# Pair 8's scores ahead of block 1's first tiles, and two pairs in a load

## The chip, the cores and the metric

The kernel runs on one core of a Trainium2 chip. The metric is the device time of one execution in microseconds. Before the change it was 324.54 us, the median of three runs (321.65, 324.54 and 325.66).

The core has five engines with an instruction queue each: TensorE (PE; its weight loads are shown apart, as PEld), VectorE (DVE), ScalarE (ACT), GpSimd (POOL) and SyncE (SP). Each runs its own instructions in order and waits on semaphores for the others. Loads from memory are issued from POOL's queue, because they turn float32 into bfloat16 on the way; stores and DMA transposes are issued from SP's.

## The reference

```python
# q, k, v: (8 batches, 8 heads, 576 positions, 64)
scores = (q @ k^T) / 8, kept where 0 <= query - key < 64, else -1e9
attn = softmax(scores)                      # rows; exp, sum, divide
x = (attn @ v) as (4608 tokens, 512)        # heads side by side
h = x @ w_in                                # w_in: 512 x 2048
g = h * clip(h + 3, 0, 6) / 6
out = g @ w_out                             # w_out: 2048 x 512; float32
```

It is a causal attention with a sliding window of 64, and behind it a two-layer network with a hard-swish between the layers.

## The kernel before, in words

**Pairs.** The attention works on pairs of heads: pair t is heads 2g and 2g+1 of batch b, with t = 4b + g, so there are 32. For a pair, `turn(t)` transposes its queries and keys on PE (36 small transposes, L276) into two PSUM banks, the "hosts"; `turned(t, 0)` copies the keys to KT on DVE and `turned(t, 1)` the queries to QT on ACT (both L283). `s_first` (L296) and `s_rest` (L310) multiply keys by queries, `s_first` into the unused end of the hosts of the next pair and `s_rest` into two banks of `ps_t`. `weights` takes the exponentials on ACT (L319, L323) and multiplies them by 0/1 masks of the window: one product into P (L328) and two into Pz (L331). From pair 8 on these products run on POOL; on pairs 4 to 7 on DVE. `pv(t)` (L404) multiplies the weights by V, with a column of ones for the sums; `pv_out(t)` divides (L413 to L428, DVE). Then `x_(t)` brings the result to xT by DMA transposes on SP (L442), or, up to pair 7, `x_turned(t)` by transposes on PE (L457, L459) and a copy on ACT (L463).

**Blocks.** The network works on blocks of 512 tokens. A block has 16 first units, each of four matmuls (L487, one for each group of 128 inputs, g = 0 to 3), a ReLU on ACT (L499) and a product on DVE (L500) that ends in gT; and 16 second units of four matmuls each (L523), every fourth with a copy on ACT (L529) and a store from SP (L531). Input group g of a block comes from the pairs with that g, so the first three matmuls of block 1's units need only pairs 4 to 6, and the fourth needs pair 7.

**PSUM banks.** `ps_t` has three banks, `ps_h` two, `ps_acc` one, and `ps_o` one tile of two banks, which `pair_bank()` also hands out. The hosts stand in `ps_h`. A new tile in a pool waits until the last reader of the tile that held its bank is done.

**The order around the change.** The order is written out by hand. Pairs 4 to 7 (batch 1) are scored and finished in two loops; pair 8's transposes follow (`turn_two(8)`), then what is left of block 0. Then comes the stretch that is changed. In the kernel before it reads: three matmuls each of block 1's units 0, 1 and 2; `x_turned(7)`; three of unit 3; the fourth matmul of all four, with their ReLU and product; then `pads(3)` (small memsets on POOL) and `group(7, 4)`. As pair 7 is finished already, `group(7, 4)` transposes pair 9, scores pair 8 and weaves in four entries of the queue `moe`: units 4, 5 and 6 and one second unit.

From pair 8 on, the loop runs `group(t, n)`: outputs of pair t, transposes of pair t + 2, scores of pair t + 1 with their exponentials and masks, and n entries of `moe`.

**Loads.** `load_qk(b, n, first)` issues a load of k and one of q for n pairs of batch b, from pair `first` on (L119, each on POOL's queue); `load_v` loads V in three parts (L138), and `shift` makes a shifted copy of V with two DMAs on SP (L158, L159). Pairs 8, 9 and 10 are loaded one by one while batch 1 is finished. Pair 11's load stands behind `group(7, 4)`, and so on POOL behind pair 8's masks; the first two parts of batch 3's V follow it. Batch 3's pairs 12 to 15 are loaded one by one behind `group(8)` to `group(11)`, that is, on POOL behind the masks of pairs 9 to 12. From batch 4 on, all four pairs come in one load. A POOL instruction that stands behind a DMA issue waits until the issue is made.

Of the kernel before, what the change touches and what calls it, by code (L numbers as in the profile page):

```python
# [36 lines left out]
def kernel(  # L37
# [10 lines left out]
    B, H, S, _ = q.shape  # L48
    DM, FF = moe_w_in.shape
    NT = B * S  # L50
    NG = H // 2
# [3 lines left out]
    NFC = FF // P  # L55
# [14 lines left out]
    ps_t = ctx.enter_context(tc.tile_pool(name="ps_t", bufs=3, space=PSUM))  # L70
    ps_h = ctx.enter_context(tc.tile_pool(name="ps_h", bufs=2, space=PSUM))
    ps_acc = ctx.enter_context(tc.tile_pool(name="ps_acc", bufs=1, space=PSUM))
# [26 lines left out]
    def load_early_qk(pairs, first=0):  # L99
        if first:  # L100
            tiles = staged[0]
        else:
            both = stage.tile([SP, 2, H, R * D], BF16, name="qk6", tag="qk")
            tiles = [both[:, 0], both[:, 1]]
        h = 2 * first
        for n in pairs:
            for t, src in zip(tiles, (q, k)):
                nc.gpsimd.dma_start(  # L108
                    out=t[:, h : h + 2 * n, :],
                    in_=src[0, h : h + 2 * n].rearrange("h (p r) d -> p h (r d)", r=R),  # L110
                )
            h += 2 * n
        return tiles

    def load_qk(b, n=NG, first=0):
        t = staged[b] if first else stage.tile([P, H, RL * D], BF16, name="qk9", tag="qk")
        hs = slice(2 * first, 2 * (first + n))
        for z, src in enumerate((k, q)):
            nc.gpsimd.dma_start(  # L119
                out=t[halves[z], hs], in_=src[b, hs].rearrange("h (p r) d -> p h (r d)", r=RL)  # L120
            )
        return t
# [8 lines left out]
    def load_v(b, whole=False, part=slice(None)):  # L131
        loads = (
            (0, Un[b % 2][:, 0], 2 * P), (2 * P, Un[b % 2][:, 1], 2 * P),
            *(((W, Us[b % 2][:, 0], 2 * P), (W + 2 * P, Us[b % 2][:, 1], 2 * P)) if whole
              else ((4 * P, Us[b % 2][3 * P // 4 : P, 1], W),)),
        )
        for m, to, n in loads[part]:
            nc.gpsimd.dma_start(  # L138
                out=to[:, :, VO : VO + P],
                in_=v[b, :, m : m + n, :].rearrange("h (p r) d -> p h (r d)", r=2),  # L140
            )
# [127 lines left out]
    def turn(t):  # L269

        b, g = divmod(t, NG)
        hosts[t] = [ps_h.tile([P, 8 * P], BF16, name=name, tag="bk") for name in ("tk", "tq")]
        for r in range(RL):
            for h in range(2):
                for z in range(2):
                    nc.tensor.transpose(  # L276
                        out=hosts[t][z][halves[h], r * W : (r + 1) * W],
                        in_=staged[b][halves[z], 2 * g + h, r * D : (r + 1) * D],
                        identity=ident[halves[z], halves[z]],
                    )  # L280

    def turned(t, z):
        (nc.scalar.copy if z else nc.vector.tensor_copy)(  # L283
            out=(QT[t % 4][:] if z else KT[t % 4][:, W:]).rearrange("q (p r) -> q p r", r=RL),
            in_=hosts[t][z][:, 0:S].rearrange("q (r p) -> q p r", p=W),
        )
# [4 lines left out]
    def s_first(t, host):  # L291

        s = [x[0:D, 6 * P : 8 * P].bitcast(F32).rearrange("p (r w) -> p r w", w=W) for x in hosts[host]]
        for r in range(2):
            for h in range(2):
                nc.tensor.matmul(  # L296
                    s[h][:, r], lhsT=keys(t, h, 0, r), rhs=QT[t % 4][halves[h], 0:W], start=True, stop=True,
                )
        return s

    def s_rest(t):

        ss = [ps_t.tile([P, 2, 2, 2, W], F32, name="s", tag="bk") for _ in range(2)]
        for c in range(2):
            for m in range(2):
                for r in range(2):
                    for h in range(2):
                        for i in range(2):
                            w = 4 * m + 2 * i + 1 + c
                            nc.tensor.matmul(  # L310
                                ss[h][halves[i], c, m, r], lhsT=keys(t, h, W * (w - 1), r),
                                rhs=QT[t % 4][halves[h], w * W : (w + 1) * W], start=True, stop=True,
                            )
        return ss
# [68 lines left out]
    def pv(t, apart=False):  # L383
        b, g = divmod(t, NG)
        if apart:
            o = [ps_h.tile([P, 512], F32, name="ot", tag="bk") for _ in range(2)]
            os_[t] = [x[:].unsqueeze(1) for x in o]
        else:
            both = ps_o.tile([P, 2, 512], F32, name="o", tag="o")
            o = [both[:, i] for i in range(2)]  # L390
            os_[t] = [both[:]]
        un, us, pw = Un[b % 2], Us[b % 2], Pw[t % 4]
        for slot in range(5):
            m, h = divmod(slot, 2)
            for r in range(2):
                c0, v0 = slot * OC + r, VO - 1 + r * (D + 1)
                for c in range(2):
                    for i in range(2):
                        if slot < 4:
                            p, vt, hh = pw[halves[i], h, c, m, r], (us if c else un)[halves[i], m], 2 * g + h  # L400
                        else:
                            p = pw[halves[i], c, 0, 0, r] if i else P0[t % 4][:, c, r]
                            vt, hh = un[halves[i], 0], 2 * g + c
                        nc.tensor.matmul(  # L404
                            o[i][halves[c], c0 : c0 + D + 1], lhsT=p, rhs=vt[:, hh, v0 : v0 + D + 1],
                            start=(r == 0), stop=(r == 1), skip_group_check=True,
                        )
# [128 lines left out]
    moe = deque()  # L536
# [22 lines left out]
    def pair_bank():  # L559
        both = ps_o.tile([P, 2, 512], F32, name="hTo", tag="o")  # L560
        return [both[:, i] for i in range(2)]

    def complete(kb, fcs, pair=()):
        unit, hidden = units[kb]
        for fc in fcs:
            unit(fc, (NG - 1,), act=fc not in pair)
            if fc in pair[1:]:
                for x in pair:
                    hidden(x)
        for _ in fcs:  # L570
            moe.popleft()
# [98 lines left out]
    staged = {0: load_early_qk((1,))}  # L670
# [64 lines left out]
    u = units[0][0]  # L735
# [16 lines left out]
    def group(t, n):  # L752

        if t >= 2 * NG:
            pv(t)
        if t + 2 < T:
            turn(t + 2)
        if t + 1 < T:
            host = t + 2
            if host >= T:  # L760
                hosts[host] = [ps_h.tile([P, 8 * P], BF16, name=name, tag="bk") for name in ("tk", "tq")]
            s = s_first(t + 1, host)
            weights(t + 1, s, s_rest(t + 1))
        if t >= 2 * NG:
            pv_out(t)
        if t + 2 < T:
            turned(t + 2, 0)
        if t >= 2 * NG:
            x_(t)
        weave(2)  # L770
        if t + 2 < T:
            turned(t + 2, 1)
        weave(n - 2)
# [6 lines left out]
    def front(t, host, muls=(nc.gpsimd,) * 3):  # L780
        s = s_first(t, host)
        weights(t, s, s_rest(t), muls)
# [54 lines left out]
    late[0] = 1  # L837
    queue_block(1)
    u, some = units[1][0], range(NG - 1)
    u(0, some, ps_t)  # L840
    u(1, some, ps_t)
    u(2, some, ps_acc)
    x_turned(n + 3)
    u(3, some, to=pair_bank()[0])
    complete(1, range(4))
    f, z = [moe.popleft() for _ in range(NFC - 4)], list(moe)
    moe.clear()
    moe.extend(f[0:3] + z[0:1] + f[3:6] + z[1:2] + f[6:] + [z[2], z[4], z[3]] + z[5:])
    pads(3, nc.gpsimd.memset)
    group(2 * NG - 1, 4)  # L850
    load_qk(2, 1, 3)
    load_v(3, part=slice(0, 2))
    for t in range(2 * NG, T):
        b, g = divmod(t, NG)
        if g == 0 and b > 2:
            queue_block(b - 1, lead=4 if b == 3 else 2)
        group(t, -(-len(moe) // (NG - g)))
        if b + 1 < B:
            if g == 0:
                staged[b + 1] = load_qk(b + 1, NG if b > 2 else 1)  # L860
            elif b == 2:
                load_qk(b + 1, 1, g)
            if b == 2 and g == 0:
                load_v(b + 1, part=slice(2, 3))
            if b > 2 and g == 1:
                load_v(b + 1)
            if g == 1 + (b > 2):
                shift(b + 1)
# [38 lines left out]
```

## Time and profile before

| | |
|---|---|
| median of three runs | 324.54 us |
| the profiled execution | 320.98 us |
| its span, first to last instruction | 319.3 us |
| mean granted clock of TensorE | 0.997 |
| two-pair loads, k and q (batch 1) | 17.5 and 18.6 us from issue to landing, among the weights' loads |
| V, 256 KB | 5.5 us, median |
| xT by DMA transpose | 2.9 and 2.4 us, median |

The KB of a load are those that it writes, in bfloat16. A row of a timeline gives the start, the time from the start to the end of the group, the engine, the line, the operation with its output and inputs, the number of instructions, and in brackets the idle time ahead of it with what ended it. Matmuls are pipelined, so rows overlap a little; the chain of waits counts each stretch of time once.

### The profile page before, as it was taken

To read this page: it belongs to the slowest core of one execution; us is meant where nothing else is said; L and a number is where in the kernel's file an instruction comes from. 1 tells how busy PE (TensorE), PEld (TensorE's weight loads), DVE (VectorE), ACT (ScalarE), POOL (GpSimd) and SP (SyncE) were. 2 spreads that over 40 slices of the span, in tenths; PEclk is the share of its full clock that TensorE was granted. 3 is DMA by queue.
4 is the path that set the end of the run, shared out by engine and by line. 5 is a ranking of instruction groups with operands and counts; after the bars stand their busy time and mean duration, and the time that the engine had idled before them with its cause. 6 is when DMAs were issued, how large, how long until landed. Compare 5 with 4: busy or idle time off the path is not lost.

```text
span 319.3 us, 10688 instructions
## 1 busy us (share of the span) xinstructions
PE 302.0 (95%) x4566; PEld 151.8 (48%) x4608; DVE 181.3 (57%) x415; ACT 184.3 (58%) x345; POOL 124.3 (39%) x168
## 2 busy tenths in 40 slices
PE   7889998998999999999999999999999999999992
PEld 3454454544555455555555555555544444444440
DVE  5766657587737754775377537762776156334200
ACT  2738575586757754776477647764773266454410
POOL 8981206289876335543445345633330000000000
PEclk9999999999999999999999999999999999999998
DMA  6999999939999943994299339934021200100021
GB/s 89 161 210 206 207 192 158 201 51 142 168 140 192 98 118 88 166 130 116 88 158 139 107 100 160 138 105 100 4 69 38 84 33 0 69 33 34 36 75 65
DMA packets 57592, 35.67 MB, mean 112 GB/s; under 512 B 39872, under 2 KB 51648, under 8 KB 57536
## 3 DMA queue, kind: packets, MB, share of 16 engines
q0 software_dynamic: 35904, 18.81, 46.0%
q1 hardware_dynamic: 21632, 16.08, 20.4%
q8 instruction: 38, 0.62, 0.8%
q14 instruction: 18, 0.15, 0.1%
HBM read 37.62 MB, written 9.44 MB: 147 GB/s over the span
## 4 chain that ended last, share of the span: by engine, by line
PE 84%; POOL 5%; DMA 3%; ACT 2%; DVE 2%; issue 2%; POOLq 0%; ACTq 0%; DVEq 0%
PE acc L523 36%; PE hT L487 35%; PE o L404 3%; PE s L310 2%; PE acco L523 2%; PE tk L276 2%; DMA V<-in_v_dram 2%; DMA qk<-in_q_dram 2%; POOL qk L108 2%; POOL Pz L331 1%; PE tq L276 1%; ACT t L499 1%; POOL V L138 1%; POOL qk L119 1%; PE hTo L487 1%
## 5 line engine op out<-in xcount | busy, mean ns | idle before, releaser
L500 DVE SCALAR_TENSOR_TENSOR gT<-t,hT 128x512 bf16<-128x512 bf16 x141 | 95.7, 687 | 78.2 <-ACT t L499 77.2
L487 PE MATMUL hT<-xT,win 128*128 128x512 bf16 x550 | 132.1, 379 | 1.8 <-DVE gT L500 0.6
L523 PE MATMUL acc<-wout,gT 128*128 128x512 bf16 x520 | 126.4, 379 | 2.2 <-issue 1.3
L499 ACT ACTIVATE t<-hT,half_const 128x512 bf16<-128x512 f32 x141 | 95.8, 690 | 48.3 <-PE hT L487 46.5
L487 PEld LDWEIGHTS <-win 128*128 128x128 bf16 x576 | 55.5, 98 | 66.6 <-issue 2.0
L523 PEld LDWEIGHTS <-gT 128*128 128x128 bf16 x576 | 54.5, 98 | 63.2
L331 POOL TENSOR_TENSOR Pz<-e,band 128x512 bf16<-128x512 bf16 x48 | 54.3, 1149 | 0.0
L328 POOL TENSOR_TENSOR P<-e,first 64x256 bf16<-64x256 bf16 x24 | 16.0, 666 | 88.7 <-ACT e L319 88.7
L529 ACT COPY osb<-acc 128x512 f32<-128x512 f32 x34 | 19.9, 586 | 43.1 <-PE acc L523 40.2
L323 ACT ACTIVATE e<-s 128x512 bf16<-128x512 f32 x56 | 30.1, 590 | 0.2 <-issue 0.2
L283 DVE COPY KT<-tk 128x576 bf16<-128x576 bf16 x28 | 21.0, 750 | 5.3 <-ACT e L319 4.5
L138 POOL DMA_DIRECT2D V<-in_v_dram x22 | 17.9, 818 | 8.8 <-DMA wout<-in_moe_w_out_dram 4.6
L428 DVE TENSOR_TENSOR opl<-o,recs 128x256 bf16<-128x256 f32 x52 | 19.7, 420 | 0.5
L283 ACT COPY QT<-tq 128x576 bf16<-128x576 bf16 x28 | 17.8, 637 | 1.5 <-PE tq L276 1.5
L413 DVE TENSOR_REDUCE sums<-o 128x10 f32<-128x20 f32 x26 | 4.6, 176 | 23.6 <-PE o L404 23.6
L404 PEld LDWEIGHTS <-Pz 64*64 64x64 bf16 x1008 | 11.5, 108 | 12.9 <-issue 9.8
L319 ACT ACTIVATE e<-tk 64x128 bf16<-64x128 f32 x28 | 7.6, 271 | 15.1 <-PE tq L296 15.1
L276 PE MATMUL tq<-ident,qk 64*64 64x64 bf16 x504 | 13.9, 195 | 0.6 <-DMA qk<-in_q_dram 0.6
L310 PE MATMUL s<-QT,KT 64*64 64x64 bf16 x896 | 14.1, 195 | 0.4 <-DVE gT L500 0.4
L404 PE MATMUL o<-V,Pz 64*64 64x65 bf16 x936 | 13.6, 195 | 0.8 <-POOL Pz L331 0.8
L276 PE MATMUL tk<-ident,qk 64*64 64x64 bf16 x504 | 14.0, 195 | 0.0
L276 PEld LDWEIGHTS <-qk 64*64 64x64 bf16 x1008 | 11.6, 106 | 2.9 <-issue 2.1
(102 smaller groups left out, 195.9 us busy)
## 6 DMA issues: line engine op xcount, KB each, us to landing
out_dram<-osb SPq DMA_DIRECT2D x36, 256.0 KB, 2.2
V<-in_v_dram POOLq DMA_DIRECT2D x16, 256.0 KB, 5.5
V<-V SPq DMA_DIRECT2D x6, 432.0 KB, 4.3
qk<-in_k_dram POOLq DMA_DIRECT2D x4, 576.0 KB, 7.0
qk<-in_q_dram POOLq DMA_DIRECT2D x4, 576.0 KB, 9.5
wout<-in_moe_w_out_dram POOLq DMA_DIRECT2D x2, 1024.0 KB, 17.3
qk<-in_q_dram POOLq DMA_DIRECT2D x12, 144.0 KB, 4.0
qk<-in_k_dram POOLq DMA_DIRECT2D x12, 144.0 KB, 4.0
```

Source lines behind the costliest of these rows:

```text
L138: nc.gpsimd.dma_start(out=to[:, :, VO : VO + P], in_=v[b, :, m : m + n, :].rearrange("h (p r) d -> p h (r d)", r=2),)
L276: nc.tensor.transpose(out=hosts[t][z][halves[h], r * W : (r + 1) * W], in_=staged[b][halves[z], 2 * g + h, r * D : (r + 1) * D], identity= ...
L283: (nc.scalar.copy if z else nc.vector.tensor_copy)(out=(QT[t % 4][:] if z else KT[t % 4][:, W:]).rearrange("q (p r) -> q p r", r=RL), in_= ...
L310: nc.tensor.matmul(ss[h][halves[i], c, m, r], lhsT=keys(t, h, W * (w - 1), r), rhs=QT[t % 4][halves[h], w * W : (w + 1) * W], start=True, ...
L323: nc.scalar.activation(out=e[:].rearrange("p c m r w -> p (c m r w)"), in_=ss[h][:].rearrange("p c m r w -> p (c m r w)"), func=EXP, scale ...
L331: muls[h].tensor_tensor(out=Pw[t % 4][:, h].rearrange("p c m r w -> p (c m) (r w)"), in0=e[:].rearrange("p c m r w -> p (c m) (r w)"), in1 ...
L404: nc.tensor.matmul(o[i][halves[c], c0 : c0 + D + 1], lhsT=p, rhs=vt[:, hh, v0 : v0 + D + 1], start=(r == 0), stop=(r == 1), skip_group_che ...
L487: nc.tensor.matmul(hT, lhsT=win16[:, g, fc * P : (fc + 1) * P], rhs=xT[:, g, t0 : t0 + TB], start=(g == 0), stop=(g == NG - 1),)
L499: nc.scalar.activation(out=t1[:], in_=hT, func=RELU, bias=half_const[:], scale=1.0 / 6.0)
L500: nc.vector.scalar_tensor_tensor(out=gT[:, fc, :], in0=t1[:], scalar=1.0, in1=hT, op0=MIN, op1=MULT)
L523: nc.tensor.matmul(acc, lhsT=gT[:, fc, ts * P : (ts + 1) * P], rhs=wout16[:, fc, :], start=(fc == 0), stop=(fc == NFC - 1),)
L529: nc.scalar.copy(out=osb[:], in_=acc)
```

## The change

Two things are moved in the program.

First, of block 1's units only unit 0 starts ahead of `x_turned(7)`, now in the pair bank; unit 1 follows it in `ps_acc`. Then pair 9 is transposed and pair 8 scored (`front(8, 9)`), and only then are units 0 and 1 completed and units 2 to 6 run whole, each with four matmuls. The second unit that `group(7, 4)` wove in is called directly. The number of units and their order in the queue behind are the same. On POOL, pair 8's masks come at the same place among the loads: behind `pads(3)`, ahead of pair 11's load.

Second, pairs 12 and 13 come in one load of k and one of q, behind `group(8)` (behind pair 9's masks), and pairs 14 and 15 in one load of each behind `group(9)`. The loads behind `group(10)` and `group(11)` are gone. The order on SP is the same.

```diff
     u, some = units[1][0], range(NG - 1)
-    u(0, some, ps_t)
-    u(1, some, ps_t)
-    u(2, some, ps_acc)
+    u(0, some, to=pair_bank()[0])
     x_turned(n + 3)
-    u(3, some, to=pair_bank()[0])
-    complete(1, range(4))
-    f, z = [moe.popleft() for _ in range(NFC - 4)], list(moe)
-    moe.clear()
-    moe.extend(f[0:3] + z[0:1] + f[3:6] + z[1:2] + f[6:] + [z[2], z[4], z[3]] + z[5:])
+    u(1, some, ps_acc)
+    turn(2 * NG + 1)
     pads(3, nc.gpsimd.memset)
-    group(2 * NG - 1, 4)
+    front(2 * NG, 2 * NG + 1)
     load_qk(2, 1, 3)
     load_v(3, part=slice(0, 2))
+    turned(2 * NG + 1, 0)
+    complete(1, range(2))
+    turned(2 * NG + 1, 1)
+    for fc, pool in zip(range(2, 7), (ps_t, ps_t, ps_h, ps_h, ps_t)):
+        moe.popleft()
+        u(fc, pool=pool)
+    f, z = [moe.popleft() for _ in range(NFC - 7)], list(moe)
+    moe.clear()
+    z.pop(0)()
+    moe.extend(f[0:3] + z[0:1] + f[3:7] + f[7:] + [z[1], z[3], z[2]] + z[4:])
     for t in range(2 * NG, T):
...
             if g == 0:
-                staged[b + 1] = load_qk(b + 1, NG if b > 2 else 1)
-            elif b == 2:
-                load_qk(b + 1, 1, g)
+                staged[b + 1] = load_qk(b + 1, 2 if b == 2 else NG)
             if b == 2 and g == 0:
                 load_v(b + 1, part=slice(2, 3))
+            if b == 2 and g == 1:
+                load_qk(b + 1, 2, 2)
```

## Prediction

> **What bounds the kernel now.** I read the page first (busy time by engine), then TensorE's waits by window, then the chain of waits and the timelines of 55 to 92 us, where the change lies, and at last the landing times of the loads.
>
> ```profile
> span 319.3 us, 10688 instructions
> ...
> PE 302.0 (95%) x4566; PEld 151.8 (48%) x4608; DVE 181.3 (57%) x415; ACT 184.3 (58%) x345; POOL 124.3 (39%) x168
> ```
>
> TensorE (PE), busy for 95% of the span, is the bound. The order of the instructions shows that it issues the same matmuls and transposes in both kernels, in another order, so all that can be won is idle time of PE; all that can be lost is new idle time. The waits of PE between 55 and 92 us, in total us, times, longest:
>
> ```profile
> PE o L404 <- POOL Pz L331: 0.8, 1, 0.8
> PE tq L276 <- DMA qk<-in_q_dram: 0.6, 1, 0.6
> PE s L310 <- DVE gT L500: 0.4, 1, 0.4
> PE hT L487 <- ACT e L323: 0.2, 1, 0.2
> PE hT L487 <- DVE gT L500: 0.2, 1, 0.2
> ```
>
> That is 2.2 us, 0.7% of the span, and the whole prize. The chain of waits says how they hang together:
>
> ```profile
> 58.51 1.94 PE hT L487 x9
> ...
> 60.95 0.65 ACT xT L463
> ...
> 67.75 1.20 POOL qk L119 x2
> 68.95 1.77 POOL V L138 x2
> 70.72 0.70 POOL P L328
> 71.42 2.21 POOL Pz L331 x2
> 73.63 0.57 POOL qk L119
> 74.20 5.21 DMA qk<-in_q_dram
> ...
> 79.46 0.21 PE tq L276
> ```
>
> From 67.75 to 79.46 the chain is not on PE: POOL has just ended pair 8's masks, issues pair 11's loads and V (2.97 us), only then masks pair 9, then issues pair 12's load, and pair 12's transposes wait for that load's q. The waits of 0.8 and 0.6 us are both this one chain; the last three belong to the block 1 tiles and the scores before it.
>
> **The change part by part.** Matmuls of PE around pairs 8 to 10, before:
>
> ```profile
> 67.99 0.45 PE L404 MATMUL o<-V,Pz 64*64 64x65 bf16 x32
> ...
> 68.34 0.19 PE L276 MATMUL tk<-ident,qk 64*64 64x64 bf16 x1
> ...
> 69.09 2.76 PE L487 MATMUL hT<-xT,win 128*128 128x512 bf16 x11
> ...
> 73.68 0.39 PE L404 MATMUL o<-V,Pz 64*64 64x65 bf16 x24 [0.78 <-POOL Pz L331]
> ...
> 78.33 0.45 PE L404 MATMUL o<-V,Pz 64*64 64x65 bf16 x32
> ```
>
> *Step 1, one unit ahead of pair 7's transposes.* Unit 0's first three matmuls now go to the bank pair that pair 7's outputs still hold; its last reader on VectorE (L428, two instructions) is the first row of the next fence: 57.73 + 0.76 = 58.49. PE comes there at 58.51, so the wait costs 0 to 0.1 us; I take 0.04 (58.55). Unit 0's three matmuls are 3 x 1.94 / 9 = 0.65, pair 7's five transposes 0.5 (58.51 + 1.94 = 60.45 to the copy at 60.95), unit 1's three 0.65: PE comes to pair 9's transposes at 60.35. Before, three units stood ahead of pair 7's transposes and a fourth ahead of pair 9's.
>
> ```profile
> 57.73 0.76 DVE L428 TENSOR_TENSOR opl<-o,recs 128x256 bf16<-128x256 f32 x2
> ...
> 68.21 0.69 DVE L500 SCALAR_TENSOR_TENSOR gT<-t,hT 128x512 bf16<-128x512 bf16 x1 [0.43 <-ACT t L499]
> ```
> ```profile
> 55.26 0.60 POOL L119 DMA_DIRECT2D qk<-in_q_dram  x1
> ```
> ```profile
> qk<-in_q_dram POOLq DMA_DIRECT2D x1, 144.0 KB, 5.8
> ```
>
> *Step 2, pair 9's transposes early: a wait is added.* Pair 9's q is issued at 55.26 and lands 5.8 later, at 61.06 (the second and third fence). Nothing ahead of it on POOL changes. So PE waits 61.06 - 60.35 = 0.7 us where it waited for nothing; bounds 0 and 1.0. Queued behind it on PE are pair 8's scores and all of block 1; ScalarE's exponentials wait with them. This is paid from the 0.8 us of the last three waits above, which go.
>
> *Step 3, pair 8's scores and the rest of block 1's first units.* Transposes with scores took 69.09 - 68.34 = 0.75, so they end at 61.81. Left before pair 8's outputs are 2 + 20 matmuls of units and 4 of the second product, 26 x 0.2156 = 5.61: 67.42, against 67.99. But now ScalarE's order counts:
>
> ```profile
> 64.35 0.27 ACT L319 ACTIVATE e<-tk 64x128 bf16<-64x128 f32 x1
> ...
> 65.62 1.44 ACT L499 ACTIVATE t<-hT,half_const 128x512 bf16<-128x512 f32 x2
> 66.96 0.63 ACT L283 COPY QT<-tq 128x576 bf16<-128x576 bf16 x1
> 67.48 0.70 ACT L499 ACTIVATE t<-hT,half_const 128x512 bf16<-128x512 f32 x1
> 68.92 0.27 ACT L319 ACTIVATE e<-tk 64x128 bf16<-64x128 f32 x1 [0.74 <-PE tq L296]
> ```
>
> Pair 8's exponentials start at about 61.45 and take 65.62 - 64.35 = 1.27; two units' ReLUs 66.96 - 65.62 = 1.34; pair 9's QT copy 67.48 - 66.96 = 0.52; the ReLUs of units 2 to 5 four times 0.67: 67.26. VectorE's product of unit 5 (0.69) ends at 67.95, and only then is the bank free that pair 10's transposes write. PE would be there at 67.42 + 0.35 (67.99 to 68.34) = 67.77; it waits 0.2 and goes on at 68.0, against 68.34 before. Gain of steps 1 to 3: 0.34 us, bounds -0.3 (the load of step 2 0.6 later) and 0.8 (no wait left).
>
> *Step 4, pair 8's masks early on POOL.*
>
> ```profile
> 84.89 0.27 ACT L319 ACTIVATE e<-tk 64x128 bf16<-64x128 f32 x1 [1.48 <-PE tq L296]
> ```
> ```profile
> 18.30 0.64 POOL L119 DMA_DIRECT2D qk<-in_k_dram  x1
> ...
> 83.43 0.65 POOL L119 DMA_DIRECT2D qk<-in_k_dram  x1
> ...
> 88.31 0.64 POOL L119 DMA_DIRECT2D qk<-in_k_dram  x1
> ```
>
> Where POOL is free, masks end 88.31 - 84.89 = 3.42 us after the exponentials start. So pair 8's end at 61.45 + 3.42 = 64.87; pair 11's loads and V (1.20 + 1.77) follow until 67.84, still ahead of pair 9's exponentials at 68.92 - 0.34 = 68.58. Pair 9's masks end at 68.58 + 3.42 = 72.0 instead of 73.63. Pair 9's outputs start at about 72.3 and no longer wait: the 0.78 us goes, and pair 10's outputs stand at 78.33 - 0.34 - 0.78 = 77.2. If something else held POOL, they would wait 0.78 again.
>
> *Step 5, two pairs in a load.* A two-pair issue took POOL 0.64 us (18.30) as a one-pair issue does (0.65 at 83.43), so issuing is free and POOL saves two pairs of issues. But pair 12's data now come with pair 13's. Pair 12's k is issued at 72.0 instead of 73.63; how much later does a q of double size land? From k's issue to q's landing one pair took 79.41 - 73.63 = 5.8 here, and 84.07 + 3.2 - 83.43 = 3.8 where the queues were emptier; four pairs took 93.82 + 10.4 - 93.09 = 11.1:
>
> ```profile
> 84.07 0.61 POOL L119 DMA_DIRECT2D qk<-in_q_dram  x1
> ...
> 93.09 0.74 POOL L119 DMA_DIRECT2D qk<-in_k_dram  x1
> 93.82 0.70 POOL L119 DMA_DIRECT2D qk<-in_q_dram  x1
> ```
> ```profile
> qk<-in_q_dram POOLq DMA_DIRECT2D x1, 144.0 KB, 3.2
> ```
> ```profile
> qk<-in_q_dram POOLq DMA_DIRECT2D x1, 576.0 KB, 10.4
> ```
>
> Between one and four pairs that is 1.8 to 2.4 us a pair: two pairs take 6.2 to 7.6; I take 6.9, the middle, since V of pair 8's time now lies further ahead of the load than before: landing 78.9. PE would be at pair 12's transposes at 77.2 + 0.35 = 77.6, so it waits 1.3 us in place of 0.6 and goes on at 78.9 instead of 79.46. [...]
>
> Pairs 14 and 15 follow pair 10's masks, which pair 10's outputs at 77.2 need, and are used behind pair 12's outputs, whose masks end at 88.31: even 11.1 us of landing is hidden. Pair 13 comes early and had no wait. The V and shift copies keep their places on their queues.
>
> *The sum.* PE goes on at 78.9 instead of 79.46 and does the same work from there on: a gain of 0.5 us in a span of 319.3. The profiled execution took 320.98 us (its span and 1.7 around it), so 320.5 for it; it stands 3.6 below the median of 324.54. I lay the difference on the median: 324.0.
>
> **The rivals.**
> (a) *All waits go.* If the two-pair load lands within 5.6 us of k's issue, nothing waits at 77.6, and the gain is 79.46 - 77.6 = 1.9: 322.7. For it: 3.8 us where the queues are emptier, and V's lead. Against: twice the bytes. Chance 0.2.
> (b) *Slower: the larger load lands later than the smaller one did.* Place: pair 12's transposes. It decides from 79.41 - 72.0 = 7.4 us on after k's issue. At 8.2 (5.8 and 2.4) the loss is 0.8: 325.3; if it landed as late as the four-pair load, 11.1, the loss is 3.7: 328.2. For it: 0.6 us of wait stood there with half the size. Against: it is issued 1.6 us earlier. Chance 0.25.
> (c) *No effect.* The wait of step 2 is 0.4 longer, pair 9's masks come no earlier than 72.4 and the landing is 7.0 later: 79.4, as before, 324.5. The early scores then only trade one wait for another. Chance 0.1.
>
> **How the numbers follow.** The forecast has 0.45, (a) 0.2, (b) 0.25, (c) 0.1. The three runs lie from 321.65 to 325.66, which is wider than all cases together, so the range is the runs' spread laid around the cases: low 321.65 - 1.4 (between forecast and (a)) = 320.2, high 325.66 + 0.5 (between no change and (b)'s first size) = 326.2. A change of 2%, 6.5 us, is about what a measurement of this kernel can tell from none. Faster by that is beyond the 2.2 us of idle time: 0.03. Slower by that needs (b) with a landing 14 us after the issue, beyond the four-pair row: 0.05. Within 2%: 0.92.
>
> **What would show it.** Step 1: pair 7's copy of xT at about 59.7 instead of 60.95. Step 2: a wait of 0.5 to 1 us of PE at L276 near 61 for the DMA of pair 9. Step 3: L404 of pair 8 near 67.5, a small wait for VectorE at L276 near 68. Step 4: no wait of L404 for POOL near 73, pair 9's masks ending near 72. Step 5: one wait at L276 for DMA of about 1.3 us, ended near 78.9. Wrong would be: no DMA wait there, one ending after 79.5, or a new wait of PE after 80 us, where I expect none.

## The result and the profile after

The changed kernel takes 325.71 us (median of 16 runs, 323.19 to 328.18), the kernel before 321.94 (median of 16 runs, 320.88 to 325.66): ratio 1.0106, 95% interval 1.0076 to 1.0136. By the ratio it is slower by 3.4 us, where 0.5 us less was forecast. The ratios here and below leave out runs more than 1.5% above the fastest of their kernel: one of these sixteen, and for the order alone three of twelve, which took 325.9 to 328.2 us at a mean clock of 0.973 to 0.982. The three runs shown with the kernel before lay high; the forecast was laid on their median.

The head of the page, and TensorE's waits between 55 and 95 us, of the kernel after:

```profile
span 322.7 us, 10730 instructions
```
```profile
PE s L310 <- issue: 3.8, 3, 2.2
PE tq L276 <- DMA qk<-in_q_dram: 1.3, 1, 1.3
```

Four of the five waits of before are gone, masks (0.8 us) among them; the fifth, for pair 12's load, has grown from 0.6 to 1.3 us. New is something that no row of before prepared for: 3.8 us in which TensorE stands still inside the scores and waits for nothing that the profile shows ("issue"). Before has one row of that name in this stretch:

```profile
PE acc L523 <- issue: 0.5, 3, 0.2
```

Each of its three stands where one of a unit's four matmuls (0.22 us) is missing from the trace (its page counts 4566 matmuls and 4608 weight loads), so it is no stop. The stops of the kernel after, in order of time:

```profile
62.68 0.35 PE L310 MATMUL s<-QT,KT 64*64 64x64 bf16 x18 [0.93 <-issue]
68.68 0.45 PE L404 MATMUL o<-V,Pz 64*64 64x65 bf16 x32
...
74.94 0.41 PE L310 MATMUL s<-QT,KT 64*64 64x64 bf16 x28 [0.69 <-issue]
...
78.84 0.45 PE L404 MATMUL o<-V,Pz 64*64 64x65 bf16 x32
...
80.71 0.21 PE L276 MATMUL tq<-ident,qk 64*64 64x64 bf16 x1 [1.33 <-DMA qk<-in_q_dram]
...
88.15 0.41 PE L310 MATMUL s<-QT,KT 64*64 64x64 bf16 x28 [2.17 <-issue]
...
92.06 0.45 PE L404 MATMUL o<-V,Pz 64*64 64x65 bf16 x32
```

This execution was already 0.62 us late at pair 4's outputs, ahead of the change. From there to pair 13's outputs it took 49.69 us (50.50 to 100.19) against 46.92 before (49.88 to 96.80): 2.8 us more. That is 3.8 of stops and 0.7 of longer DMA wait, less 1.6 of waits won (2.9 in all).

**Where the stops are.** A score has 32 matmuls in its second part, so the counts x18, x28 and x28 say that TensorE stopped 14, 4 and 4 matmuls in. I number TensorE's instructions as the program lists them, weight loads included:

```
                       first L310 matmul   matmuls done   stop behind
pair 8                 1958                14             1986
pair 10                2490                 4             2498  = 1986 + 2 x 256
pair 12                3002                 4             3010  = 1986 + 4 x 256
```

The stops are whole multiples of 256 instructions apart, and the trace itself counts 256 matmuls and 256 weight loads from each to the next. Both pages also have a DMA queue of the kind "instruction", q8, with 38 packets and 0.62 MB; TensorE's 4608 matmuls and 4608 weight loads (on the page after) are 36 times 256. The traces do not name the engine that q8 serves; that it is TensorE is read from this count and from the times below. The transfers of 85.0 to 85.5 us in the kernel after, by queue (packets, MB, share of 16 engines), show one such packet among the loads and copies:

```profile
q0 software_dynamic: 75, 0.07, 89.5%
q1 hardware_dynamic: 62, 0.02, 22.4%
q8 instruction: 1, 0.02, 16.8%
```

Going through both traces in steps of 0.5 us, there is one q8 packet for each 256 instructions in this stretch:

```
                  before                          after
boundary in    packet starts   reached      packet starts   reached   goes on
pair 8         58.5 - 59.0     63.5         59.0 - 59.5     61.6      62.68
pair 9         64.0 - 64.5     68.7         64.0 - 64.5     69.4
pair 10        70.0 - 70.5     74.3         72.5 - 73.0     74.1      74.94
pair 11        76.5 - 77.0     79.8         78.5 - 79.0     81.1
pair 12        81.5 - 82.0     84.6         85.0 - 85.5     85.8      88.15
```

Before, a packet of pairs 9 to 12 starts 0.5 to 2.7 us behind the boundary ahead of it, and TensorE reaches the next boundary 2.6 us or more after the start. After, with larger loads and V's loads at another moment, it starts 3.1 to 4.4 us behind it for pairs 10 to 12. At pair 8 TensorE comes 1.9 us sooner than before, and the packet's transfer takes 1.9 us instead of 0.9.

Two things in the traces tie the stops to these packets. First, TensorE goes on a nearly fixed time behind the end of the packet's transfer: 61.06 and 62.68, 73.46 and 74.94, 86.66 and 88.15 us in the kernel after, and 1.3 to 1.7 us in all 30 stops of 0.14 to 3.04 us that this profile and those of the experiments have between 55 and 100 us. A packet that is through by the time that TensorE comes can therefore still be too late: pair 8's ended at 61.06 us, TensorE came at 61.6 and stood until 62.68. Second, the packets start late where loads move. In the 2 us behind a boundary the loads (q0) took 0.1% and nothing of the 16 engines' time for pairs 8 and 12 in the kernel after, and the next packet started 1.5 and 1.1 us behind it; for pairs 9, 10 and 11 they took 143, 101 and 65% (above 100% where transfers overlap), and it started 3.1, 3.7 and 4.2 us behind it.

### The profile page after: what moved, and what is told of

Read it like the earlier page. It is cut to its first block, busy times and chain, and to the rows that moved or that the text cites. A ratio compares the mean times of both kernels' runs of the same rounds, so it can differ in the third digit from the quotient of the medians.

```text
span 322.7 us, 10730 instructions
## 1 busy us (share of the span) xinstructions
PE 304.4 (94%) x4608; PEld 151.4 (47%) x4608; DVE 180.9 (56%) x415; ACT 183.9 (57%) x345; POOL 121.8 (38%) x164
## 4 chain that ended last, share of the span: by engine, by line
PE 86%; DMA 4%; POOL 3%; DVE 2%; issue 2%; ACT 1%; POOLq 0%; ACTq 0%; DVEq 0%
PE acc L523 36%; PE hT L487 36%; PE o L404 3%; PE s L310 3%; PE acco L523 2%; DMA qk<-in_q_dram 2%; PE tk L276 2%; DMA V<-in_v_dram 2%; POOL qk L108 2%; PE tq L276 1%; PE hTo L487 1%; POOL Pz L331 1%; PE xp L375 0%; PE xp L459 0%; ACT xT L378 0%
## 5 line engine op out<-in xcount | busy, mean ns | idle before, releaser
L523 PE MATMUL acc<-wout,gT 128*128 128x512 bf16 x544 | 129.0, 379 | 0.0
L523 PEld LDWEIGHTS <-gT 128*128 128x128 bf16 x576 | 54.5, 98 | 63.2
```

What stands on the lines that cost most here:

```text
L523: nc.tensor.matmul(acc, lhsT=gT[:, fc, ts * P : (ts + 1) * P], rhs=wout16[:, fc, :], start=(fc == 0), stop=(fc == NFC - 1),)
```

## The experiments

Theory F: the loads crowd the DMA engines, and TensorE's instruction packets, like the data, come late. Rivals: the stops are waits for banks that the new order makes (B); only pair 12's later landing costs (L); it is the size of a single load that holds others up (S). "Before" is measured on the same chip each time.

**The order alone** (against the kernel after):

```diff
-                staged[b + 1] = load_qk(b + 1, 2 if b == 2 else NG)
+                staged[b + 1] = load_qk(b + 1, NG if b > 2 else 1)
+            elif b == 2:
+                load_qk(b + 1, 1, g)
...
-            if b == 2 and g == 1:
-                load_qk(b + 1, 2, 2)
```

> Only the new order around pair 8; the loads of batch 3 come pair by pair again, as in the kernel before. Theory F (instruction supply): TensorE's own instructions come in packets of 256 over the same 16 DMA engines as the loads, and where the loads crowd the engines the packet comes late and TensorE stands still at the first instruction of the next 256. The 2.2 us stop at pair 12's scores, which follows the load of pairs 14 and 15, should go; those at pairs 8 and 10 (0.9 and 0.7 us) may stay. Ratio 0.996 to 1.004. Rival B (banks): the stops are waits for a PSUM bank that the new order makes, so they stay where they are with the same order: ratio 1.008 to 1.011. Rival L (landing only): the loss is the later landing of pair 12's load alone, then 0.6 us goes and the rest of the loss stays, 1.007 to 1.009.

Measured: ratio 0.997 (0.9939 to 1.0001). Its waits from 55 to 95 us:

```profile
PE s L310 <- issue: 0.9, 1, 0.9
PE tq L276 <- DMA qk<-in_q_dram: 0.8, 2, 0.6
PE hT L487 <- DVE gT L500: 0.2, 1, 0.2
```

The order alone loses nothing by this ratio; with all twelve runs its mean is 0.5 us above before's. With the same order, the stops of pairs 8 and 12 are gone and pair 10's is left: not banks, so B falls. L is not yet settled, as pair 12's load is again the old one.

**The loads alone**, with the old order: the kernel before with `load_qk(b + 1, 2 if b == 2 else NG)` behind `group(8)` and `load_qk(b + 1, 2, 2)` behind `group(9)`.

> Only the two-pair loads of batch 3; the order around pair 8 is the old one. F: a stop of 1 to 2.5 us in the scores of pair 12 (or pair 11 to 13), marked as issue, and a wait of 1.5 to 2.5 us for pair 12's load: ratio 1.006 to 1.013. B: no such stop, as the order is the old one, only the longer wait for the load (about 1 us): 1.002 to 1.004. L: 1.002 to 1.005.

Measured: 1.010 (1.0067 to 1.0133), the whole loss. The stop in this profile is 0.54 us at pair 12's scores, less than F expected, and the wait for pair 12's load 0.97 and 0.68, against 0.59 before. That is 1.6 us more, half of the loss. In this profile the rest shows in the clock: 1.4 us behind these waits, from 86.3 to 89.7, the granted clock was 0.50; half of these 3.4 us, 1.7, is the most that it costs, an estimate. (It was 0.50 from 11.2 to 21.5 us too, ahead of the change; this execution is the slowest of nine.)

**The load of pairs 14 and 15 one group later:**

```diff
-            if b == 2 and g == 1:
+            if b == 2 and g == 2:
                 load_qk(b + 1, 2, 2)
```

> The changed kernel with the load of pairs 14 and 15 one group later (behind pair 11's masks instead of pair 10's), so that it no longer stands in the DMA engines together with the shifted copy of V. F: the stop at pair 12's scores shrinks from 2.2 to under 1 us: ratio 1.002 to 1.007. B and L: nothing changes, 1.009 to 1.012, as that load is waited for by nothing in either kernel.

Measured: 1.0018 (0.9989 to 1.0047). No stop at pair 12's scores is left (0.37 and 0.71 at pairs 8 and 10), though pair 14's load is now waited for, 0.85 us, and pair 12's for 1.48, as in the changed kernel (1.33). A load that nothing waited for, moved, gave back most of the loss; B and L said that nothing would change. Here L falls as the whole cause.

**The boundary moved by 64 instructions:**

```diff
-    warm(ps_h, 4, W)
+    warm(ps_h, 36, W)
```

> The changed kernel with 32 more small matmuls of the warm-up at the start (64 instructions of TensorE, 32 of them weight loads; about 1 us, of which part lies in the wait for the first load). F: every stop marked as issue moves 32 matmuls (64 instructions) ahead in the order of TensorE: from 14 matmuls into pair 8's second part of the scores to the transposes ahead of it, and from 4 matmuls into those of pairs 10 and 12 to the transposes of pairs 11 and 13, if they come at all. B: they stay at the same matmuls of the same pairs. Time: 1.008 to 1.016 by either.

Measured: 1.0131 (1.0081 to 1.0182). Its stops from 55 us on (one of 0.93 us stands at 47.09, 1.4 us behind the end of a packet and ahead of the change), and TensorE's busy time in the transposes around the last, with the count of matmuls in brackets:

```profile
75.20 0.19 PE L276 MATMUL tk<-ident,qk 64*64 64x64 bf16 x1 [0.44 <-issue]
...
81.67 0.19 PE L276 MATMUL tk<-ident,qk 64*64 64x64 bf16 x1 [0.16 <-issue]
...
89.51 0.19 PE L276 MATMUL tk<-ident,qk 64*64 64x64 bf16 x1 [3.04 <-issue]
```
```profile
86.10:86.40 0.30, 0.20 (x12) 0.20 (x13) 1.00 1.01 245
...
89.40:89.80 0.40, 0.29 (x24) 0.27 (x23) 1.00 0.95 172
```

Twelve transposes are done, 24 follow. The old place was behind 36 transposes, 4 matmuls of the first part and 4 of the second, 44; 44 - 12 = 32, the matmuls that were added. This is the clearest proof of the boundary: the order around it is the same, only the count moved. B, by which the stops would have stayed, falls here too.

**Each load of batch 3 one group earlier, with the new order** (against the order alone):

```diff
     load_qk(2, 1, 3)
+    staged[3] = load_qk(3, 1)
     load_v(3, part=slice(0, 2))
...
-            if g == 0:
-                staged[b + 1] = load_qk(b + 1, NG if b > 2 else 1)
-            elif b == 2:
-                load_qk(b + 1, 1, g)
+            if g == 0 and b > 2:
+                staged[b + 1] = load_qk(b + 1, NG)
+            elif b == 2 and g < 3:
+                load_qk(b + 1, 1, g + 1)
```

> The new order with one-pair loads, each of batch 3's loads one group earlier: pair 12's stands right behind pair 11's, behind pair 8's masks and ahead of V, pair 13's behind pair 9's masks, and so on. Nothing should then wait for a load (0.8 us of waits for pairs 9 and 13 or 12 in the order-only kernel, 0.6 of them for batch 3). Theory F: what can stay is a stop of TensorE for its own instructions at pair 10's scores, 0.5 to 1.5 us, as V's loads are issued 1.3 us later but still in front of that packet. Ratio 0.992 to 1.000. Rival L (loads waited for are the whole loss): 0.992 to 0.996.

Measured: 1.0021 (0.9988 to 1.0054), outside what both expected. No load is waited for, but the stops add up to 2.4 us (1.29, 0.29 and 0.80 at pairs 10, 11 and 12): a wait for data was turned into waits for instructions.

**The same, with V's second 256 KB one group later and its 64 KB part earlier:**

```diff
-    load_v(3, part=slice(0, 2))
+    load_v(3, part=slice(0, 3, 2))
...
-                load_v(b + 1, part=slice(2, 3))
+                load_v(b + 1, part=slice(1, 2))
```

> As the kernel with pair 12's load one group earlier, and the second 256 KB of batch 3's V goes behind pair 9's masks, the 64 KB part takes its place behind pair 8's. F: fewer packets stand before the instructions of pair 10's scores, that stop falls below 0.5 us, and nothing waits for a load: ratio 0.990 to 0.998. If a stop comes at pair 11's scores instead, 0.996 to 1.003. L: as the kernel before it in this list.

Measured: 321.41 us, 0.9956 (0.992 to 0.9991): faster than both kernels, by 0.9 us against before. In the profile only 0.14 us of a stop is left at pair 10's scores and none at those of pairs 11 and 12. One of 0.54 us stands at pair 8's, and one of 1.05 us at pair 13's scores, three matmuls in, which is the 256th instruction behind 3010.

**A load that nothing reads, in the kernel before:**

```diff
                 load_qk(b + 1, 1, g)
+                if g == 1:
+                    for z, src in enumerate((k, q)):
+                        nc.gpsimd.dma_start(
+                            out=spare[halves[z]], in_=src[3, 4:8].rearrange("h (p r) d -> p h (r d)", r=RL)
+                        )
```

> The kernel before with a load added that nothing reads: pairs 14 and 15's k and q into a spare tile, issued behind pair 13's load (behind pair 10's masks), two more issues on GpSimd. No wait for a load is added, TensorE's order is untouched. F: the added bytes keep TensorE's next instructions waiting, a stop marked as issue of 0.5 to 2.5 us in the scores of pair 11 or 12: ratio 1.003 to 1.012. Rivals L and B: nothing waits for that load, and the masks of pair 11 come at most 0.3 us later: 0.999 to 1.002.

Measured: 1.0202 (1.0156 to 1.0247), far more than either expected, and at another place: no stop in the scores, but pair 14's transposes (the line is one higher here) wait for their load, and then the clock falls (the share granted is the third figure from the right):

```profile
94.54 0.26 PE L277 MATMUL tk<-ident,qk 64*64 64x64 bf16 x1 [5.08 <-DMA qk<-in_k_dram]
```
```profile
94.00:95.00 1.00, 0.26 (x1) 0.12 (x1) 0.00 (x0) 0.00 (x0) 0.00 (x0) 0.58 1.21 122
95.00:97.00 2.00, 1.60 (x72) 1.37 (x74) 1.58 (x5) 1.08 (x4) 0.50 (x1) 0.50 1.14 287
97.00:99.00 2.00, 2.00 (x6) 0.76 (x5) 0.28 (x1) 0.97 (x2) 2.00 (x3) 0.50 0.88 148
99.00:101.00 2.00, 2.00 (x6) 0.72 (x5) 0.00 (x0) 0.00 (x0) 1.77 (x3) 0.50 0.24 17
```

Pair 14's load, k and q of 144 KB each, landed in 3.0 and 3.2 us before, and in 10.4 and 10.3 here. With the added bytes it was data that came late, 5.08 us of waiting, and not TensorE's instructions; F had the cause and not the victim.

**The same bytes at the same places, one pair in a load** (against the kernel after):

```diff
-                staged[b + 1] = load_qk(b + 1, 2 if b == 2 else NG)
+                staged[b + 1] = load_qk(b + 1, 1 if b == 2 else NG)
+            if b == 2 and g == 0:
+                load_qk(b + 1, 1, 1)
...
-                load_qk(b + 1, 2, 2)
+                load_qk(b + 1, 1, 2)
+                load_qk(b + 1, 1, 3)
```

> The changed kernel with the same pairs loaded at the same places, but one pair in a load: pairs 12 and 13 as four issues behind pair 9's masks, 14 and 15 as four behind pair 10's. F: the same bytes stand before the instructions, so the stop at pair 12's scores stays (1 to 3 us); pair 12's own load lands earlier, so the wait for it falls from 1.3 to about 0.7 us: ratio 1.005 to 1.010. Rival S (it is the size of a single load that holds the others up): the stop goes, 0.998 to 1.003.

Measured: 1.001 (0.9971 to 1.0048), as S said; but the stops in its profile are 4.0 us, as F said. Nothing waits for a load. A second profile, with the changed kernel on the same chip, and each half of the edit by itself:

> The kernel with the same bytes in one-pair loads a second time: its profiled execution took 1.2 us more than the median of its runs, so another profile should show less of the stops than 4.0 us, 1.5 to 3.5 in all. Ratio 0.998 to 1.005.

> The changed kernel a second time, on the chip of the next three. F: stops marked as issue at the same places (4 matmuls into the second part of pair 10's or 12's scores, 14 into pair 8's), 2 to 4.5 us in all, with other lengths than in the first profile, and a wait of 1.0 to 1.6 us for pair 12's load. Ratio 1.007 to 1.014.

> The changed kernel, where only pairs 14 and 15 are loaded one by one (at the same place); pairs 12 and 13 come in one load. F with S (a two-pair load holds up what stands behind it more than two one-pair loads of the same bytes): the stop at pair 12's scores shrinks, the wait for pair 12's load stays at 1.0 to 1.6 us: 1.001 to 1.005. Rival L (the wait for pair 12 and the dip of the clock behind it are most of the loss): 1.007 to 1.011.

> The changed kernel, where only pairs 12 and 13 are loaded one by one; pairs 14 and 15 come in one load. L: the wait for pair 12's load falls below 0.7 us and most of the loss goes with it: 1.000 to 1.004. F with S: the stop of 2 us at pair 12's scores stays: 1.005 to 1.009.

```
                                  median   ratio (interval)           stops   mean clock
all four pairs one by one         322.78   1.0019 (0.999 to 1.0048)   2.8     0.9938
changed kernel                    325.10   1.0082 (1.0053 to 1.0112)  2.0     0.9893
only 14 and 15 one by one         323.74   1.0053 (1.0026 to 1.008)   2.9     0.9929
only 12 and 13 one by one         325.65   1.0089 (1.0056 to 1.0121)  3.6     0.9882
kernel before                     321.94                              -       0.9943
```

Stops are us in one profiled execution, the clock is the mean over 12 runs (35 of before). The stops do not order the times; the clock does better. Neither half's profile has a wait for pair 12's load, though 1.0 to 1.6 us was expected with 14 and 15 alone one by one; with 12 and 13 alone one by one the kernel loses as much as the changed one without that wait, against L. The changed kernel's second profile has one stop, pair 12's, and waits of 0.88 us for pair 12's load, and of 1.5 us for pair 9's, which the first had not.

In that profile the clock fell three times, first from 8.6 to 12.0 us, ahead of the change, and twice in this stretch, here behind the stop of 2.02 us that ended at 89.31:

```profile
88.00:89.00 1.00, 0.00 (x0) 0.00 (x0) 1.00 (x3) 0.00 (x0) 0.66 (x1) 1.00 1.13 44
89.00:90.00 1.00, 0.53 (x29) 0.51 (x30) 0.30 (x1) 0.17 (x1) 0.00 (x0) 1.00 0.22 42
90.00:91.00 1.00, 1.00 (x5) 0.39 (x4) 0.00 (x0) 1.00 (x3) 0.50 (x1) 0.77 0.72 135
91.00:92.00 1.00, 1.00 (x4) 0.40 (x3) 0.00 (x0) 0.93 (x2) 1.00 (x2) 0.50 0.09 16
92.00:93.00 1.00, 1.00 (x4) 0.30 (x2) 0.00 (x0) 0.00 (x0) 0.76 (x1) 0.50 0.01 1
93.00:94.00 1.00, 1.00 (x4) 0.37 (x3) 0.00 (x0) 0.00 (x0) 0.00 (x0) 0.53 0.57 211
```

From 90.5 to 94 TensorE has its work, at a granted clock of 0.50: by the clock 0.23 + 0.5 + 0.5 + 0.47 = 1.7 us lost, an estimate, nearly as much as the stop itself. The other fall came behind 1.5 us of waiting for pair 9's load at 61.3 to 63.0 (0.85 and 0.67, the wait of step 2). Of the changed kernel's 12 runs here the four with a mean clock of at least 0.994 take 323.9 us, and before's 26 such runs 321.9, so I put 2.0 us down to idle time. The mean over all runs is 325.3 against 322.2, and another 1.1 us of the 3.1 goes with the clock. Both are estimates, as a fall ahead of the change counts in them too. The first profile of the kernel after, with no fall in this stretch, shows the idle part alone.

## Why the prediction was wrong

- *Step 1* was right: pair 7's copy comes at 60.53, which without the 0.62 us of late start is 59.9 (forecast 59.7).
- *The waits of before* left out a row, the 0.5 us of "issue" at L523. That cost nothing, as it stands for missing records.
- *Step 2*: the wait for pair 9's load has its place. In the first profile the late start hid it; in the second it was 1.5 us, above the bound of 1.0.
- *Step 3* missed the gain of 0.34: pair 8's outputs stand 18.18 us behind pair 4's, before 18.11, as the packet's stop of 0.93 us took it. In the order-only profile they stand at 17.44, a gain of 0.67. The small wait for VectorE at pair 10's transposes came in neither.
- *Step 4* was right: with the new order no profile has the masks' wait of 0.8 us; with the old order all three have it.
- *Step 5* was wrong in size, as the next two rows show: q lands 73.64 + 7.0 = 80.64, 7.7 us behind k's issue at 72.97, where 6.9 was taken and 7.6 was the bound. That the wait is 1.3 us, as forecast, is luck: the landing and TensorE both came 1.7 to 1.8 us later than in the forecast. The wait ended at 80.71, behind the 79.5 that was named as a sign of being wrong.

```profile
72.97 0.68 POOL L119 DMA_DIRECT2D qk<-in_k_dram  x1
```
```profile
qk<-in_q_dram POOLq DMA_DIRECT2D x1, 288.0 KB, 7.0
```

- **The step that failed** is in step 5 and the sum: "even 11.1 us of landing is hidden" for pairs 14 and 15, and "does the same work from there on". Their data were in time. Their bytes were not free: they kept TensorE's own instructions waiting for 2.2 us at pair 12's scores, and behind long waits the clock fell (to 0.50, behind the 2.02 us of the second profile). I priced a load by who waits for its data alone. The stops of 0.93 and 0.69 us at pairs 8 and 10 had no term in the sum either. The range took in the result, but by luck: its upper end is the highest of three scattered runs. Rival (b) had the sign, but its mechanism, pair 12's landing, is the smaller part: with that landing at 1.48 us of wait and the last load moved, the kernel is within 0.5% of before.
- The bound "all that can be lost is new idle time" failed too: in the second profile the work behind the stop of 2.02 us went at a clock of 0.50, an estimated 1.7 us more.

**Open** is why two loads of one pair do less harm than one of two pairs with the same bytes: their stops in single profiles (4.0 and 2.8 us) are no shorter than the changed kernel's (3.8 and 2.0), the falls of the clock are fewer, and two profiles of each cannot say what decides that. A part is plain: their profiles wait for no load, where the changed kernel's wait 1.3 and 2.4 us. That loads in the engines make a packet start late is read from the times above and from the moved load; the traces do not show in which order an engine takes up its packets.

## What to carry to other kernels

A load has two prices: who waits for its data, and what comes late while its bytes are in the DMA engines. Here that was the instructions of a busy engine (2.17 us at pair 12's scores, with no stop there once the load of pairs 14 and 15 was moved) and another load's data (5.08 us with the load that nothing reads). Where many small matmuls use up 256 instructions in some 5 us (4.8 to 5.6 from boundary to boundary in the kernel before), look for idle time marked "issue" at equal distances in the program, and try loads spread out rather than joined (here 1.0019 one by one against 1.0082 in twos). Read the granted clock behind every long idle stretch on TensorE: behind one of 2.02 us it was 0.50 for 3.4 us, by estimate 1.7 us more, and behind one of 3.04 us it did not fall.

## What the hardware showed that I had not expected

In the kernel after, TensorE's stops lay whole multiples of 256 of its instructions apart, with one q8 packet to each 256 in this stretch; in all profiles, between 55 and 100 us, they lasted 0.14 to 3.04 us. The granted clock fell to 0.50 for about 3.4 us behind idle stretches of 1.5 to 2 us (twice in one execution, the changed kernel's second profile, and once in another, with the loads alone), for 6.8 us at the end of one of 5.1 us (the load that nothing reads), and not at all behind one of 2.17 (the kernel after) and one of 3.04 (the boundary moved). In the changed kernel's second profile the falls begin at 8.62, 63.23 and 90.54 us, 54.61 and 27.31 us apart. What decides whether the clock falls behind an idle stretch is not shown: the two without a fall are longer than those of 1.5 to 2 us that had one.
